# Gate and up projections in turn on chunks of 1024 tokens, in a transformer block on one Trainium2 core

## The chip, the cores and the metric

The kernel runs on one core of a Trainium2 chip (one of eight). A core has TensorE (matmuls, in the profile PE for the matmuls and PEld for their weight loads), VectorE (DVE), ScalarE (ACT), GpSimd (POOL) and SyncE (SP), which here issues all DMAs. TensorE writes only to PSUM, eight banks of 512 fp32 columns on 128 partitions; VectorE and ScalarE read them ("evict" them) into SBUF. The metric is the device time of one execution in microseconds; the median of three runs is given, and one more execution is profiled.

## What is computed

```python
xn = layernorm(x)                               # x: 2048 tokens x 576
q, k, v = xn @ wqkv                             # 32 heads of 18
s = sliding_window_attention(q, k, v, W=256) @ wo   # causal, window of 256, softmax
g = silu(((xn @ w_gate) * (xn @ w_up)) @ w_down)    # 4608 hidden columns, no nonlinearity between
return x + s * g
```

All inputs and outputs are fp32. The bilinear GLU (gate, up, their product "h", down) is the largest part of the work.

## The kernel before

**Numbers.** Each fp32 operand of a matmul is split into a high and a low fp16 part (`hi` at line 192 on ScalarE, `lo` at 195 on VectorE), and a product is three passes: high x high, high x low, low x high.

**Prologue** (up to about 179 us). Layer norm, the transposed tokens `XT`, v, then q and k; work for the loop's first weights is placed between these at negative "places".

**The loop.** 18 groups `g` of 256 hidden columns, times 4 chunks `c` of 512 tokens, make 72 slots (`NSLOT`); a slot `sl` is (g, c) and has 16 places. `seven_place(sl, place)` issues `SEVEN_N[place]` gate and up matmuls, and then `at_place` issues whatever else is due at that place. Everything else stands in the table `AT`: for each kind of step the place (counted from the first slot of the group, or from the slot), which may exceed 15 and then falls into a later slot. Each engine runs its instructions in the order in which they are issued, so the table is the schedule. Nothing is reordered at run time; an instruction that waits holds up what stands behind it on its engine, and on SP's queue a DMA that waits holds up the DMAs behind it. In one place scores come first, then down, then the rest (`RANK`).

**Gate and up by seven products.** For a 2 x 2 arrangement (two halves of the hidden columns, two halves of the tokens, two halves of the contraction) the four blocks of the result are made of seven products instead of eight (a Strassen-Winograd scheme). Weight sums are made on GpSimd (`t_sum`, line 504) and split into `TW`; sums of the tokens are made once in `s_steps` (line 536, places `AT['sx']`) into `SX` and `XD`. The units go in the order 0, 2, 1, 3, 4, 5, 6; unit 1 accumulates on the bank of 0, unit 3 on 2, 5 on 3, 6 on 4, so that a pair of banks "up" serves in turn. After each unit its bank is read (`seven_read`, line 1198): units 0 and 1 by a ScalarE copy (`seven_copy`, 1141), the others by a VectorE addition to an earlier result (`seven_add`, 1144). A unit on the same bank cannot begin before that read. The contraction of 576 leaves a tail of 64 rows; the low passes of the tails are matmuls of half the rows, two side by side (`seven_half`, 1125, at places 6 and 13).

Within a slot, a token half is 256 tokens, and each unit treats both kinds: gate in columns 0 to 255 of the bank, up in columns 256 to 511:

```python
o = slice(256 * kind, 256 * kind + 256)
nc.tensor.matmul(CH[q][:, o], a, b, start=CH["first"], ...)
```

So a matmul has 256 columns, and a slot has 92 of them, and eight of half height. At the end of a slot `seven_mult` (1148) multiplies gate by up, for each half of the hidden columns one 128 x 512 product (one on GpSimd, one on VectorE by `AT['en']`); `h_hi` (1015, ScalarE) and `h_lo` (1020, VectorE) split it, and `down` (1027) multiplies it by w_down in the next slot, in five steps of six 512-column matmuls or 24 of 64 columns, each with a VectorE addition into `acc`.

**Beside it**, slots 1 to 64 each carry one step of the attention (two heads, 512 queries): loads (`load_k`, `load_q`, `load_v`), scores (912), a masked maximum on VectorE (923), exponentials on ScalarE (935), low parts on GpSimd or VectorE (944, by `AT['en']`), a transposing DMA (947) and the weighing (956). In each group the next group's weights are loaded (`ffn_raw`, 416), their squares summed on ScalarE (`ffn_amax`, 427), the 128 partial sums spread to all partitions through DRAM (`ffn_spread_out` 436, `ffn_spread_in` 439, `ffn_scale` 447), and the weights scaled and split (`up_hi`, `up_lo`, `t_hi`, `t_lo`, `wd_*`, `dn_*`). Rings: `upw` 4 buffers, `upv` 5, `tw` 5, `hh` 4.

**End.** After slot 71 the last `down`, then `o_out` (1264) for 16 token tiles: silu, the attention's output product with wo, the product of both, the residual, the store.

## Time and profile before

| | us |
|---|---|
| median of 3 runs (1565.97 to 1566.42) | 1566.4 |
| profiled execution, its own time | 1565.05 |
| its span, first to last instruction | 1563.3 |
| busy: TensorE | 1550.1 (99%) |
| weight loads | 1107.8 (71%) |
| VectorE | 1259.1 (81%) |
| ScalarE | 1061.9 (68%) |
| GpSimd | 796.5 (51%) |
| granted TensorE clock | 1.00 throughout |

The span is from the first to the last instruction; the execution's own time has what lies around it. TensorE's busy share counts overlapping matmuls' modelled ends, so it says little of itself; the chain of waits and the waits by engine say what the end hangs on. In a row of groups stand line, engine, operation, what is written and read, shapes, count, then busy us and mean ns, then the engine's idle time just before and what ended it.

### The profile page before, as it was taken

How to read it: one execution, taken by the hardware profiler on the slowest of the kernel's cores; microseconds unless marked ns; L12 is line 12 of the kernel's file. 1: busy time of each engine (PE TensorE's matmuls, PEld its weight loads, DVE VectorE, ACT ScalarE, POOL GpSimd, SP SyncE). 2: the span in 40 equal slices, each digit the busy share in tenths (PEclk: the TensorE clock that was granted, in tenths of full speed). 3: DMA queues.
4: the chain of work that ended last, by engine and by line, in shares of the span. 5: the costliest groups of instructions: out<-in, count | busy, mean ns of one | idle time of the engine just before them, and what ended most of it. 6: DMA issues, size and time to landing. Idle time of an engine off the chain costs nothing.

```text
span 1563.3 us, 40073 instructions
## 1 busy us (share of the span) xinstructions
PE 1550.1 (99%) x15498; PEld 1107.8 (71%) x15498; DVE 1259.1 (81%) x2773; ACT 1061.9 (68%) x1854; POOL 796.5 (51%) x1015
## 2 busy tenths in 40 slices
PE   8999999999999999999999999999999999999999
PEld 5465577777777777777777777777777777777767
DVE  7536698889798989888989888888989898977655
ACT  6534487777777778787787877877778787852230
POOL 4115445546464747575756565565757474732000
PEclk9999999999999999999999999999999999999999
DMA  8683436565656686777877686877696867651238
GB/s 222 201 252 130 164 68 141 95 132 98 135 101 142 124 150 129 146 140 137 148 131 148 118 165 113 164 113 159 118 152 127 160 122 155 123 97 39 63 87 218
DMA packets 566575, 212.14 MB, mean 136 GB/s; under 512 B 504560, under 2 KB 544624, under 8 KB 566384
## 3 DMA queue, kind: packets, MB, share of 16 engines
q1 hardware_dynamic: 566384, 209.58, 64.4%
q8 instruction: 121, 1.98, 0.6%
q14 instruction: 70, 0.57, 0.1%
HBM read 76.63 MB, written 29.00 MB: 68 GB/s over the span
## 4 chain that ended last, share of the span: by engine, by line
PE 95%; DVE 1%; ACT 1%; DMA 0%; issue 0%; SPq 0%; DVEq 0%
PE up L1176 46%; PE dn L1039 25%; PE pv L956 5%; PE s L390 4%; PE up L1129 3%; PE s L912 2%; PE s L1039 2%; PE s L1279 2%; PE up L1279 2%; PE up L390 1%; PE s L341 1%; PE pv L390 1%; PE dn L390 1%; PE up L341 0%; DMA pt<-pp 0%; PE dn L341 0%
## 5 line engine op out<-in xcount | busy, mean ns | idle before, releaser
L1039 PE MATMUL dn<-dnw,hh 128*128 128x512 f16 (+1 forms) x3168 | 442.6, 286 | 0.0
L1176 PEld LDWEIGHTS <-tw 128*128 128x128 f16 x3456 | 318.1, 97 | 52.7 <-issue 4.4
L1039 PEld LDWEIGHTS <-hh 128*128 128x128 f16 x3456 | 223.2, 98 | 163.3 <-issue 19.2
L1146 DVE SCALAR_TENSOR_TENSOR gt<-up,gt 128x512 f32<-128x512 f32 x360 | 247.5, 687 | 78.2 <-PE up L1129 56.2
L1046 DVE SCALAR_TENSOR_TENSOR acc<-dn,sc,acc 128x512 f32<-128x512 f32 x310 | 215.2, 694 | 90.9 <-PE dn L1039 86.4
L931 ACT ACTIVATE mx<-mx,sig 128x2 f32<-128x2 f32 x256 | 98.1, 383 | 209.1 <-DVE mx L923 208.4
L1176 PE MATMUL up<-XT,upw 128*128 128x256 f16 x1872 | 238.6, 273 | 0.0
L1176 PE MATMUL up<-XT,tw 128*128 128x256 f16 x1728 | 234.8, 272 | 3.4 <-DVE gt L1146 3.4
L1176 PE MATMUL up<-sx,tw 128*128 128x256 f16 x1728 | 223.0, 272 | 0.0
L1176 PEld LDWEIGHTS <-upw 128*128 128x128 f16 x1872 | 178.2, 98 | 27.0 <-issue 0.2
L1151 POOL TENSOR_TENSOR ht<-gt 128x512 f32<-128x512 f32 x72 | 94.6, 1314 | 103.8 <-DVE gt L1146 102.7
L956 PEld LDWEIGHTS <-pt 128*128 128x128 f16 x2880 | 114.5, 96 | 41.8 <-DMA pt<-pp 1.6
L1176 PEld LDWEIGHTS <-upv 128*128 128x128 f16 x1152 | 105.6, 98 | 37.2 <-issue 22.0
L517 POOL TENSOR_TENSOR raw<-raw 128x256 f32<-128x256 f32 x136 | 116.6, 857 | 24.7 <-DVE upv L196 16.7
L956 PE MATMUL pv<-vt,pt 128*128 128x37 f16 x2880 | 117.8, 179 | 0.7 <-DMA pt<-pp 0.7
L1142 ACT ACTIVATE gt<-up 128x512 f32<-128x512 f32 x144 | 84.1, 584 | 49.1 <-PE up L1176 34.4
L1176 PE MATMUL up<-sx,upv 128*128 128x256 f16 x864 | 112.6, 273 | 0.0
L1017 ACT ACTIVATE hh<-ht 128x512 f16<-128x512 f32 x72 | 45.0, 625 | 37.9 <-POOL ht L1151 37.9
L196 DVE SCALAR_TENSOR_TENSOR tw<-raw,sc,tw 128x512 f16<-128x512 f32 x68 | 67.9, 999 | 0.0
L193 ACT ACTIVATE tw<-raw,sc 128x512 f16<-128x512 f32 x68 | 46.8, 712 | 27.9 <-POOL raw L517 27.9
L318 ACT ACTIVATE upw<-raw 128x1280 bf16<-128x1280 f32 (+1 forms) x51 | 62.8, 1232 | 0.5
L912 PE MATMUL s<-ks,qs 54*128 54x384 f16 (+2 forms) x512 | 60.1, 312 | 0.0
(1373 smaller groups left out, 2980.0 us busy)
## 6 DMA issues: line engine op xcount, KB each, us to landing
raw<-in_B_w_down_dram SPq DMA_DIRECT2D x36, 288.0 KB
qk_d<-qp SPq DMA_DIRECT2D x18, 512.0 KB
raw<-in_B_w_gate_dram SPq DMA_DIRECT2D x36, 256.0 KB
raw<-in_B_w_up_dram SPq DMA_DIRECT2D x36, 256.0 KB
ks<-qk_d SPq DMA_DIRECT2D x96, 81.0 KB
qs<-qk_d SPq DMA_DIRECT2D x128, 54.0 KB
vt<-v_d SPq DMA_DIRECT2D x48, 111.0 KB
qk_d<-qp SPq DMA_DIRECT2D x20, 256.0 KB
```

The lines of the kernel that those rows point to most:

```text
L196: nc.vector.scalar_tensor_tensor(w, rv, s, h, op0=OP.mult, op1=OP.subtract)
L390: nc.tensor.matmul(ps, a, b, start=i == 0 and not opened, stop=i == 12 and opened)
L517: nc.gpsimd.tensor_tensor(to, x0, x1, op=OP.subtract)
L912: nc.tensor.matmul(ps[:, :hi_ - lo_], QS[s][r, i * 128:(i + 1) * 128], KS[s][r, lo_:hi_], start=True, stop=True)
L931: nc.scalar.activation(mx[:, 1], mx[:, 0], AF.Identity, bias=sig[:, 2:3], scale=sig[:, 1:2])
L956: nc.tensor.matmul(PVB[s][:, j, i, :VW], pt[:, nb * j + n + n // nb * nb], VT[s][:, lo_ + n % nb, j * VW:(j + 1) * VW], start=n == 0, stop ...
L1039: nc.tensor.matmul(to, a, b, start=q == 0, stop=q == len(l) - 1)
L1046: nc.vector.scalar_tensor_tensor(d, src, SC[g][:, 9:10], d, op0=OP.mult, op1=OP.add)
L1142: nc.scalar.activation(seven_new(sl, name), CH[q], AF.Copy, scale=H_SC)
L1146: nc.vector.scalar_tensor_tensor(seven_new(sl, name), CH[q], H_SC, x, op0=OP.mult, op1=OP.add)
L1151: eng.tensor_tensor(HT[sl, f], u[:, 0], u[:, 1], op=OP.mult)
L1176: nc.tensor.matmul(CH[q][:, o], a, b, start=CH["first"], stop=last and q not in (1, 2, 5), skip_group_check=q in ON)
```

## The change

A slot is now (g, w, kind): a chunk `w` of 1024 tokens, and either gate (even slots) or up (odd slots). There are still 72 slots of 16 places. A token half is 512 tokens, so that a matmul has 512 columns and takes a whole bank for one kind; a slot has 46, and four of half height. A gate slot leaves its four result blocks ("11", "t", "u", "v", each 128 x 512) in tiles of their own; the up slot of the same chunk reads its block "11" from PSUM with one VectorE operation that scales it and multiplies it by the gate's (`seven_fuse`), and the other three are multiplied in SBUF (`v` and `u` on GpSimd, `t` on VectorE). `h_hi` and `h_lo` work on the four blocks; both 512-token chunks of `w` are ready after the up slot, and their downs come in the next slot (the second) and the one after (the first). After the last slot ten down steps are left.

The token sums of both 512-token parts of a 1024-token chunk go into one tile. Rings: `upw` 3, `upv` 4, `tw` 4, `hh` 5. The table `AT` has new places almost everywhere; those of which the prediction speaks are shown.

```diff
-          'en': ((0, 1, 0, 0, 0, 0, 1, 0, 0, 0), (0, 1, 0, 0, 0, 1, 1, 0, 0, 0), (0, 1, 0, 0, 0, 0, 1, 0, 0, 0),
+          'en': ((0, 1, 0, 0, 0, 0, 1, 1, 0, 0), (0, 1, 0, 0, 0, 1, 1, 0, 0, 0), (1, 1, 0, 0, 0, 0, 1, 1, 0, 0),
-          'amax': (20, 20, 13),
+          'amax': (19, 30, 6),
-          'down': ((6, 9, 12, 15, 20), (6, 8, 11, 14, 16), (6, 8, 11, 14, 16), (6, 9, 12, 15, 19)),
+          'down': ((6, 9, 12, 16, 20), (6, 8, 11, 19, 16), (6, 8, 11, 14, 16), (6, 10, 12, 15, 18)),
+          'down_last': ((11, 11, 12, 13, 11), (2, 3, 4, 5, 9)),
-          'h': (((15, 17), (18, 21)), ((17, 17), (19, 21)), ((15, 17), (21, 21)), ((15, 17), (19, 21))),
-          'load': (8, 3, 15),
+          'h': (((17, 20), (15, 16), (17, 21), (19, 20)), ((13, 14), (16, 16), (16, 18), (19, 20))),
+          'h_last': ((17, 18), (18, 19)),
+          'load': (8, 10, 15),
+          'me': (0, 1, 0),
-          'mult': {1: 6, 4: 20, 5: 1, 6: 0},
+          'mult': {4: 1, 5: 1, 6: 1},
-          'raw': (11, 11, 12, 13, -9, 2),
-          'scale': (24, 26, 36, 51),
+          'raw': (8, 10, 21, 22, -8, 0),
+          'scale': (30, 31, 38, 50),
-          't_hi': ((54, 57), (58, 65)),
-          't_lo': ((58, 59), (64, 70)),
+          't_hi': ((57, 70), (61, 74)),
+          't_lo': ((59, 73), (70, 77)),
...
-    def h_ring():
-        return post.tile([128, 2, 512], F16, name="hh", bufs=4)
+    def h_ring():
+        return post.tile([128, 2, 512], F16, name="hh", bufs=5)
...
-    def x_block(c, i, j, low):
+    def x_block(w, i, j, low, half=None):
         k = 2 * j + 5 * low
-        return XT[:, k:k + 2, c * 512 + i * 256:c * 512 + i * 256 + 256]
+        a, n = w * 1024 + i * 512, 512
+        if half is not None:
+            a, n = a + 256 * half, 256
+        return XT[:, k:k + 2, a:a + n]
...
+            for c, b in ((2 * w + 1, b + 1), (2 * w, b + 2)):
+                for n in range(5):
+                    at(min(b, NSLOT), AT["down_last"][c % 2][n] if b >= NSLOT else AT["down"][b % NCH][n], down, g, c, n)
...
+    FI = {"11": (0, 0), "t": (0, 1), "u": (1, 0), "v": (1, 1)}
...
+    def seven_half(g, c, kind, pair, stop):
+        for q, s in zip(pair, stop):
+            _, _, w, x = seven_tail(g, c, q, kind)
+            nc.tensor.matmul(CH[q], w, x, start=False, stop=s, skip_group_check=q in ON)
...
+    def seven_fuse(q, name):
+        nc.vector.scalar_tensor_tensor(GT[name], CH[q], H_SC, GT[name], op0=OP.mult, op1=OP.mult)
...
+    def seven_mult(sl, name, eng):
+        eng.tensor_tensor(GT[name], GT[name], SV[name], op=OP.mult)
...
     def seven_place(sl, place):
-        g, c = divmod(sl, NCH)
+        g, c, kind = sl // 4, sl // 2 % 2, sl % 2
...
-            o = slice(256 * kind, 256 * kind + 256)
-            nc.tensor.matmul(CH[q][:, o], a, b, start=CH["first"], stop=last and q not in (1, 2, 5),
+            nc.tensor.matmul(CH[q], a, b, start=CH["first"], stop=last and q not in (1, 2, 5),
...
+        elif q == 1:
+            if kind:
+                seven_fuse(q, "11")
+            else:
+                seven_copy(kind, q, "11")
...
-    SEVEN_N = (4, 8, 7, 6, 5, 5, 5, 4, 5, 5, 4, 6, 7, 7, 7, 7)
+    SEVEN_N = (2, 4, 4, 3, 2, 3, 2, 2, 2, 3, 2, 3, 4, 3, 4, 3)
...
-    at(NSLOT, 2, o_out, 0)
+    at(NSLOT, 8, o_out, 0)
```

More of the change, by code (lines that the diff above doesn't have):

```diff
@@ L134, in up_ring @@
     def up_ring():
-        return ring.tile([128, 10, 128], F16, name="upw", bufs=4)
+        return ring.tile([128, 10, 128], F16, name="upw", bufs=3)
     def up_ring2():
-        return ring.tile([128, 6, 128], F16, name="upv", bufs=5)
+        return ring.tile([128, 6, 128], F16, name="upv", bufs=4)
     def dn_ring():
@@ new lines @@
+    for g in range(NG):
+        for w in range(2):
+            b = 4 * g + 2 * w + 1
+            for n, name in enumerate(("v", "t", "11", "u")):
+                last = b == NSLOT - 1 and n > 1
+                for f, p in zip((h_hi, h_lo), AT["h_last"][n - 2] if last else AT["h"][w][n]):
+                    at(b, p, f, g, w, name)
+            for c, b in ((2 * w + 1, b + 1), (2 * w, b + 2)):
+                for n in range(5):
+                    at(min(b, NSLOT), AT["down_last"][c % 2][n] if b >= NSLOT else AT["down"][b % NCH][n], down, g, c, n)
```

193 lines of the change are left out of this document (89 added, 104 removed), and 30 rows, old and new, of the table AT.

## The prediction

> **What bounds the kernel now.** I read the busy shares first, then the waits of TensorE between 208 and 1480 us (the loop), then the waits of the whole span.
>
> ```profile
> span 1563.3 us, 40073 instructions
> PE 1550.1 (99%) x15498; PEld 1107.8 (71%) x15498; DVE 1259.1 (81%) x2773; ACT 1061.9 (68%) x1854; POOL 796.5 (51%) x1015
> ...
> PE pv L956 <- DMA pt<-pp: 0.7, 1, 0.7
> ...
> PE up L1176 <- DVE gt L1146: 3.4, 4, 2.1
> ```
>
> A busy TensorE proves little, since the ends of matmuls are modelled. The wait rows say more: the first, of the loop alone, is its only one, 0.7 us in 1272 us. The second is of the whole span: 3.4 us in four waits for VectorE, which lie in the opening, below. So inside the loop TensorE is the bound, and a change there is worth what it takes from TensorE's own row of instructions, unless it brings a wait. How tight that row is packed shows in the chain of waits (start, duration, what, count); the first line is from the q/k projection, the rest from the loop:
>
> ```profile
> 149.76 11.22 PE s L390 x52
> ...
> 406.72 0.33 PE up L1129 x4
> ...
> 444.62 1.29 PE dn L1039 x6
> ...
> 447.11 0.70 PE dn L1039 x24
> 447.81 3.93 PE up L1176 x36
> 451.74 0.32 PE up L1129 x4
> 452.06 0.17 PE s L912 x4
> 452.23 1.40 PE dn L1039 x6
> ...
> 479.46 0.33 PE up L1129 x4
> ```
>
> A 512-column matmul takes 11.22 us / 52 = 215.8 ns (1.29 / 6 = 215 says the same, coarser); a 256-column one 3.93 us / 36 = 109.2 ns. Two narrow ones cost 218.4 ns, so **a narrow pair costs 2.6 ns more than one wide matmul**. Read as columns plus a constant, c x 256 + k = 109.2 and c x 512 + k = 215.8: k is 2.6 ns per instruction. A weight load is not in it: 64-column matmuls with a load each follow at 0.70 / 24 = 29 ns, so a load of 128 columns fits into 29 ns and lies wholly under 109. From the halves at 406.72 to those at 479.46 are four slots: 18.2 us a slot, 1.14 us for each of its 16 places.
>
> **The change on TensorE.** The loop's up and gate instructions, counted by their weight loads:
>
> ```profile
> L1176 PEld LDWEIGHTS <-tw 128*128 128x128 f16 x3456 | 318.1, 97 | 52.7 <-issue 4.4
> ...
> L1176 PEld LDWEIGHTS <-upw 128*128 128x128 f16 x1872 | 178.2, 98 | 27.0 <-issue 0.2
> ...
> L1176 PEld LDWEIGHTS <-upv 128*128 128x128 f16 x1152 | 105.6, 98 | 37.2 <-issue 22.0
> ```
>
> With the 144 of wd (two a slot) that is 6624, 92 for each of 72 slots, as the old SEVEN_N sums to. The new one sums to 46, each of 512 columns. The half-height tails (L1129) go from four to two a call; four take 0.32 us, of which two pairs side by side are 2 x 109 and some 0.1 us is the exposed load on entering half-height rows. That 0.1 stays (the same two halves are entered), a pair becomes one of 215.8 instead of 218.4. So a slot saves (46 + 2) x 2.6 = 125 ns, and 72 slots **9.0 us**; with k taken as 2.4 or 2.8, the rounding of those rows, 8.3 to 9.7. Nothing lies over it: TensorE waits for nothing in the loop, so it comes off the end, as long as nothing else becomes late. The halved weight loads are worth nothing more, being covered by matmuls; their cover doubles.
>
> The Trainium skill ("TensorE: Matmul & The Clock Gate", section Back-to-back issue gap) gives an isolated gap of N/2.4 + 2.5 ns, near these rows, but says that a sustained stream runs at some 131 ns for N = 512; by that the sum would be 46 x (218.4 - 131) x 72 = 289 us instead of 9.0, and the row of 215.8 in a stream of 52 speaks against it.
>
> **The other engines.** Durations from the groups of 280 to 1240 us, and the load of four slots:
>
> ```profile
> L1146 DVE SCALAR_TENSOR_TENSOR gt<-up,gt 128x512 f32<-128x512 f32 x258 | 177.3, 687 | 54.4 <-PE up L1129 40.8 <-PE up L1176 7.0
> ...
> L1151 POOL TENSOR_TENSOR ht<-gt 128x512 f32<-128x512 f32 x52 | 68.7, 1322 | 27.0 <-DVE gt L1146 26.2
> L1142 ACT ACTIVATE gt<-up 128x512 f32<-128x512 f32 x104 | 60.6, 583 | 6.1 <-PE up L1176 6.1
> ...
> L1151 DVE TENSOR_TENSOR gt<-gt 128x512 f32<-128x512 f32 x52 | 41.7, 802 | 0.0
> ...
> L1023 DVE SCALAR_TENSOR_TENSOR hh<-hh,gt 128x512 f16<-128x512 f16 x52 | 35.5, 682 | 0.0
> ...
> L1017 ACT ACTIVATE hh<-gt 128x512 f16<-128x512 f32 x52 | 32.1, 617 | 0.0
> L318 ACT ACTIVATE upw<-raw 128x1280 bf16<-128x1280 f32 x26 | 33.0, 1268 | 0.4
> ...
> L944 POOL TENSOR_TENSOR pp<-sm__13529,pp 128x384 f16<-128x384 f32 x2 | 1.8, 938 | 3.5 <-DVE gt L1146 3.5
> ...
> 425.58 0.41 DVE L944 TENSOR_TENSOR pp<-sm__5965,pp 128x256 f16<-128x256 f32 x1
> ...
> 400.00:472.60 72.60, 72.60 (x769) 53.50 (x767) 61.57 (x146) 53.87 (x100) 39.12 (x56) 1.00 0.57 116
> ```
>
> Per group (four slots): evictions by addition stay 20. ScalarE copies go from 8 to 6 (-1.2 us). Products go from 4 on VectorE and 4 on GpSimd to 2 and 4, and 2 fused evictions come in, priced like the addition with the same operand places, 0.69: VectorE -1.6 + 1.4. Two subtractions of probabilities move from GpSimd to VectorE; the row at 425.58 (0.41 us for 256 columns) bounds a 384-column one between 0.4 and the 0.94 of GpSimd, I take 0.6: +1.2. VectorE goes from 61.6 to about 62.6 of 72.6 us. None of this is on TensorE's path by itself. What counts is where it stands. The fused eviction comes at place 6 of an up slot, behind the addition of unit 2, where ScalarE copied before. Its bank is wanted by unit 4, after unit 3. Cover on TensorE from the end of the halves: scores 0.17, down 1.40, unit 3 at 6 x 0.216 = 1.30, together 2.9 us; VectorE needs 2 x 0.6 (start to start, rows 185.38 and 185.98 below) = 1.2. So VectorE may come 1.7 us late before TensorE waits. Does it come late? The "L1129" part of the first row above (40.8 us, in this loop 53 slots) says no: VectorE stands idle waiting for the halves, some 0.8 us a slot. I cost the fuse at nothing; without the cover it is 0.6 an up slot, 22 us in all.
>
> The down products of a pair of 512-token blocks wait for the up slot and are issued one and two slots later. From the multiplied "v" and "t" (places 12 to 14) through ScalarE 0.6 and VectorE 0.7 to the first down at place 22 lie some eight places, 9.1 us: nothing. The raw ring of weights shrinks by one buffer each; a gate's buffers are read last in the third slot and the up weights are formed in the group's first gate slot (last low part at place 77, first use after 80, 3.4 us): nothing, while VectorE keeps within that.
>
> **The spread of the scales.** Its write is issued at place 30, right behind the last square sum (before: 24, sums at 20), the read at 31 (before 26), the reduction on VectorE at 38 (before 36).
>
> ```profile
> 421.63 0.38 SPq L178 DMA_DIRECT2D sd_f<-am  x1
> 424.19 0.34 SPq L444 DMA_DIRECT2D upv<-sd_f  x1
> 432.42 0.67 DVE L449 TENSOR_REDUCE sc<-upv 128x3 f32<-128x384 f32 x1
> SPq L444 <- DMA sd_f<-am: 45.5, 16, 4.0
> ```
>
> The read waits for the write on SP's queue, 2.8 us each (45.5 / 16), now with more of it in front of the probabilities' transposes and key loads queued behind; those at places 34 and later have slack of several places to their weighing. Place 30 to 38 is 9.1 us; square sum 1.27, write 2.6 (421.63 to 424.19), and the read may take from 2.6, as the write does, to 8.2 (the distance kept before). I take the low end, being the nearest like transfer: 6.5 of 9.1 us. At the high end (12.1) VectorE would stand 3.0 us. The raw loads move on the same queue, gate's to places 8 and 10, up's to 21 and 22, and stay 8 to 9 places ahead of their sums (before 7 to 9); query loads go from place 3 to 10 of the slot before, with 12 places (13.7 us) left to the scores, over the 8.2: nothing.
>
> **Opening and end.** Slots 0 and 1 now hold one gate and one up of 1024 tokens, with no down at all; before, slot 1 had one.
>
> ```profile
> 179.88 1.29 DVE L382 SCALAR_TENSOR_TENSOR qp<-s,qp 128x512 f16<-128x512 f32 x2 [1.67 <-ACT qp L381]
> 181.08 0.81 DVE L196 SCALAR_TENSOR_TENSOR dnw<-raw,sc,dnw 128x576 f16<-128x576 f32 x1
> ...
> 185.38 0.69 DVE L1146 SCALAR_TENSOR_TENSOR gt<-up,gt 128x512 f32<-128x512 f32 x1
> 185.98 0.68 DVE L562 TENSOR_TENSOR dnw<-dnw,XT 128x512 f32<-128x512 f32 x1
> ...
> 183.74 0.27 PE L1129 MATMUL up<-XT,upv 64*128 64x256 f16 x1
> 186.12 1.47 PE L1176 MATMUL up<-XT,tw 128*128 128x256 f16 x12 [2.11 <-DVE gt L1146]
> ...
> 189.60 1.47 PE L1176 MATMUL up<-XT,tw 128*128 128x256 f16 x12 [0.70 <-DVE gt L1146]
> ...
> 199.79 1.14 PE L1176 MATMUL up<-XT,tw 128*128 128x256 f16 x9 [0.28 <-DVE gt L1146]
> ...
> 157.18 1.30 POOL L517 TENSOR_TENSOR rqk<-raw 128x256 f32<-128x256 f32 x1
> ```
>
> Here VectorE is the bound: TensorE waits 2.11 + 0.70 + 0.28 = 3.1 us for it. I laid the new places out by hand at 0.60 an operation. Slot 0: two qp and two dnw low parts (2.7), one wd (0.4), one upv (0.5), one sx (0.6) stand before the addition of unit 2, so it starts about 184.1 against 185.4, and unit 3 near 184.8: some 1.1 us of waiting in the slot instead of 2.8. Slot 1: 14 operations of 0.6, and 4.6 of shorter ones and scores, make 13.0 us against 10.7 of TensorE: some 2.5 us of waiting, where before it was 0.3. Together 3.6 against 3.1; I take the difference as **0**, with -3 (all waiting gone) and +6 (GpSimd late in slot 0 with four t sums and four sx sums, at up to 1.3 each by the last row, before what the up slot reads) as ends.
>
> At the end two blocks' downs instead of one follow the last slot. TensorE's sum is the same; the last "u" needs 0.7 + 1.3 + 0.6 + 0.7 = 3.3 us to be ready, under four downs of block 3 (5.2 us). Zero.
>
> Sum: the profiled execution's 1565.05 us (span 1563.3 and 1.75 around it) - 9.0 = 1556.1. The runs' median, 1566.4, lies 1.35 above that execution, so **1557.4 us**.
>
> **Rivals.**
> - *VectorE becomes the bound in up slots.* Place 6 there holds addition, fused product and first down eviction. If VectorE comes over 1.7 us late, unit 4 waits for the fuse; 0.6 to 1 us in each of 36 slots is +22 to +36, and the time 1566.4 - 9.0 + 22 = 1579 or more. For: it is busy 85% of the loop. Against: it idles for the halves each slot now. It decides from 0.25 us an up slot (9.0 / 36). Chance 0.07.
> - *The scales come late.* With a read of 8.2 us VectorE stands 3.0 us at place 38, 1.7 of them covered: 1.3 x 17 = +22 - 9, 1566.4 + 13 = 1579; it decides from 1.7 + 0.5 us of lateness, where the 9.0 are gone (0.5 x 17). Chance 0.06.
> - *The opening gets longer*: +6 us, 1563.4. For: VectorE is the bound there and slot 1 loses its downs. Chance 0.10.
> - *The pair isn't dearer in the loop*, the 2.6 ns being lost in work beside it (weight loads crossing from other lines): 1566.4. Against: the x36 keep their rate between two lines' work. Chance 0.06.
>
> **How the numbers follow.** The forecast has 0.71; its own range is 1554 (opening cleared, 3 us less) to 1562 (half the opening's risk and a few scattered waits). Measurement can't tell 0.2%, 3.1 us, from no change. The opening's case, 3.0 us faster, lies on that border; I count 0.02 of it as faster. Faster: 0.71 + 0.02 = 0.73. Same: the other 0.08 and the no-gain case's 0.06 = 0.14. Slower: 0.07 + 0.06 = 0.13. The range for 8 in 10 reaches up through the opening and no-gain cases, 1553.5 to 1566.5, leaving out the slower ones.
>
> **What would show it.** The chain of a middle slot should show up matmuls at 0.216 us (x18 in 3.88), PEld about 3600 fewer instructions, and VectorE still waiting for the halves. TensorE's waits between 208 and 1480 should stay near 1 us. Wrong would be: a wait of TensorE on the fused eviction once an up slot; VectorE waiting for the spread's DMA; over 6 us of waits in the opening.

## The result, and the profile after

The changed kernel takes **1582.7 us** (median of four runs, 1581.0 to 1586.1) against 1566.2 for the kernel before, run beside it: a ratio of 1.0109 (95% interval 1.0092 to 1.0127). It is slower by 16.5 us, where 9 us less were forecast. The profiled execution has a span of 1581.2 us (before 1563.3).

The page of the changed kernel, span and busy times:

```profile
span 1581.2 us, 32793 instructions
...
PE 1549.4 (98%) x11898; PEld 769.9 (49%) x11898; DVE 1267.6 (80%) x2803; ACT 1047.0 (66%) x1818; POOL 761.7 (48%) x985
```

There are 3600 weight loads fewer, as forecast. Its chain of waits in a middle slot (start, duration, what, count):

```profile
448.57 3.88 PE up L1184 x18
452.45 0.32 PE up L1134 x2
```

That is 215.6 ns for a matmul of 512 columns, and 0.32 us for the halves: **TensorE's gain is there**. Start to start, without waits, the 3312 wide matmuls take 715 us where the 6624 narrow ones took 723, and the halves some 0.5 us less: 8.8 us together. But TensorE now waits. Its waits in the loop (208 to 1480 us; engine, line, what it waits for: us in total, times, longest):

```profile
PE pv L964 <- DMA pt<-pp: 11.2, 15, 2.3
PE up L1184 <- ACT gt L1148: 5.0, 17, 1.6
```

Before, the one such row held 0.7 us. The first row is the weighing of probabilities, waiting for a transposing DMA; the second a gate matmul whose bank ScalarE has not yet copied. The same view of 178 to 222 us, the opening, whose total was 3.1 us before and is 5.7 now (it overlaps the first: the wait of 1.6 us, at 210.9, is in both, so that 16 of the 17 belong to the loop's later groups):

```profile
PE up L1184 <- ACT gt L1148: 1.6, 1, 1.6
PE up L1184 <- DVE gu L1157: 1.4, 2, 0.9
PE up L1184 <- DVE uu L1157: 1.2, 1, 1.2
PE up L1184 <- DVE gv L1157: 1.1, 1, 1.1
```

These rows leave out waits that the trace does not put down to anyone. So I also took, for every neighbouring pair of matmuls, the distance of their starts less the distance that the same pair has where nothing waits, and added up what is left (from 40 ns on; from here on, "by starts"). By this the waits are 5.4 us before (3.5 in the opening, 1.0 in the loop, 0.9 at the end) and 31.2 after (7.5, 22.8, 0.9). 1563.3 - 8.8 + 25.8 = 1580.3, against a span of 1581.2: **the account closes to 1 us**, and the same sum gives the span of every experiment below that keeps TensorE's full clock to 2.5 us or better. The loop's waits stand in three places of each group of four slots:

| where | count, us | released by |
|---|---|---|
| third slot, weighing of the third query block | 12, 10.4 | transposing DMA |
| first slot, unit 1 (and small ones beside it) | 28, 7.0 | ScalarE's gate copy |
| first slot, weighing of the third block, and in four groups unit 3 | 10, 4.8 | transposing DMA, VectorE |

How the third-slot wait comes about shows in the chain of waits from 425 to 441 us:

```profile
430.08 1.69 POOL gu L1160
431.77 0.96 SPq L955
...
432.85 0.50 SPq L907
...
433.46 0.43 SPq L447
...
433.99 0.39 SPq L1001
...
434.48 3.99 DMA pt<-pp
...
438.51 0.47 PE pv L964 x12
```

GpSimd's product of "u" (1.69 us) stands ahead of a low part of the probabilities, for which the second transpose waits on SP's queue (L955); behind it in the same queue stand a load of v (L907), the read of the spread (L447) and a store (L1001), and only then the third transpose, whose transfer takes 3.99 us. The weighing is 0.66 us late.

And VectorE, from the middle of a group's last slot (first row) through the first half of the next group's first slot (second row); stretches in us, then their length and the busy time of PE, PEld, DVE, ACT and POOL. First the changed kernel, then the kernel before at the same point of a group:

```profile
757.69:766.98 9.29, 9.29 (x69) 4.25 (x67) 9.19 (x22) 8.16 (x15) 6.93 (x9) 1.00 0.66 143
766.98:775.82 8.84, 8.61 (x85) 4.32 (x84) 8.84 (x14) 7.74 (x14) 7.75 (x8) 1.00 0.57 113
```

```profile
753.00:762.33 9.33, 9.33 (x90) 6.24 (x89) 9.30 (x22) 6.93 (x12) 8.36 (x10) 1.00 0.63 115
762.33:772.07 9.74, 9.74 (x120) 7.64 (x119) 8.41 (x17) 7.38 (x15) 4.05 (x6) 1.00 0.99 175
```

VectorE was full at the end of a group before, too (9.30 of 9.33), but then had room (8.41 of 9.74) to catch up. Now it is full for the next half slot as well (8.84 of 8.84), while GpSimd works 7.75 us of it instead of 4.05.

### The profile page after: what moved, and what is told of

The parts are those of the page before. It is cut to its first block, busy times and chain, and to the rows that moved or that the text cites. A ratio compares the mean times of both kernels' runs of the same rounds, so it can differ in the third digit from the quotient of the medians.

```text
span 1581.2 us, 32793 instructions
## 1 busy us (share of the span) xinstructions
PE 1549.4 (98%) x11898; PEld 769.9 (49%) x11898; DVE 1267.6 (80%) x2803; ACT 1047.0 (66%) x1818; POOL 761.7 (48%) x985
## 4 chain that ended last, share of the span: by engine, by line
PE 73%; DVE 11%; DMA 6%; issue 3%; ACT 2%; POOL 2%; SPq 1%; DVEq 0%; ACTq 0%; POOLq 0%
PE up L1184 33%; PE dn L1046 18%; DMA pt<-pp 5%; PE pv L964 4%; PE s L393 4%; DVE hh L1031 3%; PE up L1134 2%; PE s L1046 2%; PE s L1292 2%; PE s L920 2%; PE up L1292 2%; PE up L393 1%; DVE gt L1160 1%; DVE acc L1053 1%; PE pv L393 1%
## 5 line engine op out<-in xcount | busy, mean ns | idle before, releaser
L1184 PE MATMUL up<-XT,upw 128*128 128x512 f16 x936 | 238.8, 379 | 5.2 <-ACT gt L1148 5.0
L1184 PE MATMUL up<-XT,tw 128*128 128x512 f16 x864 | 232.3, 378 | 4.2 <-DVE gu L1157 1.4
L1184 PE MATMUL up<-sx,tw 128*128 128x512 f16 x864 | 222.9, 378 | 0.1
L1184 PEld LDWEIGHTS <-tw 128*128 128x128 f16 x1728 | 147.4, 97 | 142.6 <-issue 9.1
L1184 PEld LDWEIGHTS <-upw 128*128 128x128 f16 x936 | 86.6, 98 | 102.6 <-issue 10.4
L964 PE MATMUL pv<-vt,pt 128*128 128x37 f16 x2880 | 120.5, 179 | 11.4 <-DMA pt<-pp 11.2
L1184 PE MATMUL up<-sx,upv 128*128 128x512 f16 x432 | 111.3, 381 | 0.0
L1160 POOL TENSOR_TENSOR gv<-gv,uv 128x512 f32<-128x512 f32 x36 | 53.5, 1487 | 62.4 <-DVE uv L1157 62.4
L1184 PEld LDWEIGHTS <-upv 128*128 128x128 f16 x576 | 49.2, 97 | 69.4 <-issue 22.1
L1160 POOL TENSOR_TENSOR gu<-gu,uu 128x512 f32<-128x512 f32 x36 | 47.5, 1320 | 19.6 <-DVE uu L1157 14.8
L1157 DVE SCALAR_TENSOR_TENSOR uu<-up,ut 128x512 f32<-128x512 f32 x36 | 24.9, 692 | 39.6 <-PE up L1134 21.6
L1134 PE MATMUL up<-XT,upv 64*128 64x512 f16 x144 | 55.7, 386 | 0.1
```

The source lines that it names most:

```text
L964: nc.tensor.matmul(PVB[s][:, j, i, :VW], pt[:, nb * j + n + n // nb * nb], VT[s][:, lo_ + n % nb, j * VW:(j + 1) * VW], start=n == 0, stop ...
L1134: nc.tensor.matmul(CH[q], w, x, start=False, stop=s, skip_group_check=q in ON)
L1160: eng.tensor_tensor(GT[name], GT[name], SV[name], op=OP.mult)
L1184: nc.tensor.matmul(CH[q], a, b, start=CH["first"], stop=last and q not in (1, 2, 5), skip_group_check=q in ON)
```

## The experiments

All are compared with the kernel before, run on the same chip beside them; the ratio is to that. The last two columns are TensorE's waits in us by starts, in the opening and in the loop.

| kernel | us | ratio (95%) | opening | loop |
|---|---|---|---|---|
| the changed kernel | 1582.7 | 1.0109 (1.0092 to 1.0127) | 7.5 | 22.8 |
| t's low part first | 1587.8 | 1.0147 (1.0130 to 1.0164) | 7.1 | 25.7 |
| attention's old places | 1603.6 | 1.0249 (1.0234 to 1.0264) | 10.4 | 42.3 |
| sum of squares earlier | 1578.7 | 1.0086 (1.0068 to 1.0104) | 10.1 | 16.3 |
| weighing later | 1574.0 | 1.0056 (1.0040 to 1.0072) | 7.3 | 13.2 |
| last slot relieved | 1578.3 | 1.0081 (1.0065 to 1.0096) | 7.3 | 17.3 |
| these last three | 1576.4 | 1.0070 (1.0052 to 1.0088) | 9.3 | 14.5 |
| weighing later, t earlier | 1574.6 | 1.0057 (1.0042 to 1.0072) | 7.1 | 14.3 |
| and last slot relieved | 1574.3 | 1.0057 (1.0042 to 1.0072) | 7.1 | 14.5 |
| opening's work ahead | 1576.0 | 1.0066 (1.0051 to 1.0081) | 6.0 | 18.6 |
| weights' sums later | 1578.4 | 1.0086 (1.0069 to 1.0103) | 7.2 | 18.8 |
| product apart, weighing later | 1585.4 | 1.0124 (1.0109 to 1.0139) | 7.3 | 24.6 |
| and sums later, opening | 1574.1 | 1.0051 (1.0034 to 1.0068) | 6.6 | 15.1 |
| and one low part behind | 1572.7 | 1.0047 (1.0033 to 1.0060) | 8.1 | 12.3 |

### Two suspects: the low part of t, and the sum of squares

```diff
-  'h': (..., ((13, 14), (16, 16), (16, 18), (19, 20))),
+  'h': (..., ((13, 17), (15, 15), (16, 18), (19, 20))),
```

> Edit: in odd chunks the split of block t (high part and low part, places 16 and 16) is done at place 15, ahead of v's low part (14, now 17). Nothing else moves. Theory 'two regular waits': in the first slot of each group TensorE waits 0.38 us (17 times, 6 us) for the gate's copy of unit 0, because its single tile is freed only by t's low part, which stands in VectorE's line behind v's; the waits should vanish and the time fall from 1582.7 to about 1577. Rival 'VectorE is the bound': its line is simply full there, the wait goes to the next bank that it reads, and the time stays within 1.5 us of 1582.7.

1587.8 us, slower still. The loop's waits now begin with:

```profile
PE up L1184 <- DVE gu L1157: 15.5, 17, 1.1
```

The 17 waits for the gate copy are gone (one of them is left), and 17 of 0.9 us stand at the next thing that VectorE owes TensorE, the read of unit 2: the wait was passed on. It also grew, by starts from 0.37 to 1.09 us a group; where the difference comes from is seen under "The wait that moves".

```diff
-  'amax': (19, 30, 6),  'scale': (30, 31, 38, 50),  'up_hi': (41, 54, 45, 60),  'up_lo': (44, 57, 50, 65),
+  'amax': (19, 34, 6),  'scale': (34, 35, 43, 50),  'up_hi': (44, 54, 46, 60),  'up_lo': (47, 57, 50, 65),
```

> Edit: the square sum of the up weights goes from place 30 to 34, the spread's write and read from 30 and 31 to 34 and 35, the reduction from 38 to 43, the first two weight splits after it 3 places later. Theory 'two regular waits': the sum stands in ScalarE's line between a score maximum and its exponentials in the second slot of each group, and the spread's write, waiting for it, holds the transposes behind it on SP's queue, so that the weighing in the third slot finds its transposed probabilities late (12 waits, 10.3 us). Those waits go, time about 1573 to 1575. Rival 'GpSimd's products': the low parts are late since u's product (1.7 us) stands ahead of them on GpSimd; then the waits stay and the time is within 2 us of 1582.7. Rival 'the wait moves': the sum now delays the exponentials of the slot after, and new waits of the same size show up one slot later.

1717.7 us, 1.096 (with the exchange of the low parts as well 1721.9, 1.100). In both one low part of gate's first weights is formed from raw weights that the first sum has already overwritten, with the same instructions. The chain of one third slot:

```profile
703.26 1.36 ACT upw L321 x2
...
704.64 2.29 DMA sd_f<-am
...
706.94 0.33 SPq L447
...
707.38 5.98 DMA pt<-pp
...
715.44 2.13 PE up L1184 x5
```

Sum of squares, write of the spread, read behind it on SP's queue, and only then the transpose that the weighing wants: four places later brought 65 us of waiting for transposes. (The last row is of the last section.) So the order of these on SP's queue can set the time; but so large a shift does not say that it does in the changed kernel. The combination says nothing more:

> Edit: e1 and e2 together. Theory 'two regular waits': their gains add up, 6 + 8 to 10 us, time about 1567 to 1569; the rest over the forecast of 1557.4 is the opening (4 us) and the late transposes in first slots (4 us). Rival 'VectorE is the bound': at most the larger one of the two gains shows.

### Attention's new places

Rows 'p' and the engines 'en' of the kernel before, in the changed kernel:

> Edit: the places of the attention's steps and the engine of their low parts are put back to those of the kernel before; all else as in the changed kernel. Theory 'two regular waits': the transposes are late for the square sum's sake and not for their own places; the waits in the third slot of each group stay, time within 3 us of 1582.7. Rival 'later transposes': the new places (second transpose 15 instead of 13, third 20 instead of 19, with the weighing where it was) made them late; the waits go, time about 1572.

1603.6 us. The waits for transposes stay (9.8 us), but the time does not, as the first theory had it, stay within 3 us: 32 waits for gate copies come to 23.0. The new places are not the fault; the old ones fit this order of work worse.

### Where the third slot's wait can be taken away

```diff
-  'raw': (8, 10, 21, 22, -8, 0),   'amax': (19, 30, 6),  'scale': (30, 31, 38, 50),
+  'raw': (8, 10, 17, 17, -8, 0),   'amax': (19, 24, 6),  'scale': (26, 29, 38, 50),
```

> Edit: up's raw weights are loaded at place 17, their square sum stands at place 24 (30 in the changed kernel) and the write and read of the spread at 26 and 29 (30 and 31); the scales are still reduced at 38 and nothing else moves. Theory A (the late square sum stands in ScalarE's line ahead of the exponentials, and its write holds up SP's queue ahead of two transposes): the twelve waits of the weighing in the third slots, 10.3 us, fall below 3 us, SP's waits for the square sum (17.6 us) fall below 6, and the time is 1573 to 1576. Theory B (the third transpose is late because of VectorE and GpSimd, the spread is not in it): the weighing's waits stay above 8 us and the time is 1580 to 1584. The gate copy's 17 waits (5.0 us) stay under both.

1578.7 us. Of the twelve waits in third slots two are left (1.0 us), with three in second slots (1.6), as theory A had it. SP's waits, first of the changed kernel (for the square sum and for the spread's write), then of this one:

```profile
SPq L181 <- ACT upw L321: 17.6, 13, 4.5
SPq L447 <- DMA sd_f<-am: 8.6, 7, 1.8
```

```profile
SPq L447 <- DMA sd_f<-am: 14.9, 15, 2.0
SPq L181 <- ACT upw L321: 11.7, 11, 2.5
```

The longest wait for the square sum falls from 4.5 to 2.5 us, and the third transpose is in time, although SP waits longer for the write. SP's total for the square sum, 11.7 us, is not below the 6 that theory A named, and the time is above its 1573 to 1576: in the first group the earlier loads and sums fall into the opening, which waits 2.6 us more.

```diff
-  (13, 14, 15, 18, 24), (13, 14, 16, 20, 24), ...   # 'p', second slots: weighing of n = 4, 5
+  (13, 14, 15, 18, 26), (13, 14, 16, 20, 27), ...
-  (13, 14, 15, 19, 26), (13, 14, 15, 21, 26), ...   # fourth slots
+  (13, 14, 15, 19, 27), (13, 14, 15, 21, 28), ...
```

> Edit: only the weighing of the third query block (n = 4, 5) moves, from places 24, 24 to 26, 27 in steps of the second slots, and from 26, 26 to 27, 28 in steps of the fourth. Theory A (a transpose comes a fixed 0.5 to 2.4 us too late for one place in the order): the weighing's waits of 14 us fall below 4 us, and the time is 1572 to 1575. Theory B (lateness is passed on: the place is late because everything behind it is late): the waits turn up again at the weighing of the last block or at the read of the result, the sum of loop waits stays above 19 us and the time above 1579. The gate copy's waits (5.0 us) stay under both.

1574.0 us, theory A: 8.7 us for moving only where TensorE takes up what comes late. Of the weighing's 11.2 us by the profile 0.6 is left, and the gate copy's row is as it was (5.0 us, 17):

```profile
PE pv L964 <- DMA pt<-pp: 0.6, 1, 0.6
```

### VectorE's line at the end of a group

Low parts of next weights out of the last slot's end:

```diff
-  'dn': ((45, 45), (48, 55), (54, 49)),  'up_hi': (41, 54, 45, 60),  'up_lo': (44, 57, 50, 65),
+  'dn': ((45, 45), (46, 47), (54, 49)),  'up_hi': (41, 48, 45, 54),  'up_lo': (44, 50, 53, 57),
```

> Edit: four of VectorE's subtractions and two of ScalarE's roundings for the next group's weights move out of the end of the group's last slot, where VectorE has no gap from place 8 of that slot to place 10 of the next: both low parts of w_down to 46 and 47 (48, 55), up's two weight pairs rounded at 48 and 54 (54, 60), with low parts at 50 and 57 (57, 65), one of gate's at 53 (50). No work is added or left out. Theory A (VectorE's line is full there, and the gate copy's wait for the buffer that the low part of t reads is its backlog): the 17 waits of unit 1 (6.5 us start to start) fall below 2 us, waits of the weighing in first slots (3.9 us) fall by half, and the time is 1573 to 1577. Theory B (the buffer's order alone makes that wait): the 17 waits stay at 0.3 us or more each and the time is 1581 to 1585.

1578.3 us, 4.4 less than the changed kernel. The gate copy's waits in first slots fall only from 7.0 to 4.7 us, and 16 new ones, 3.8 us, stand at the beginning of the fourth slot, where the moved low parts now are. The weighing's fall by 5.8. Neither theory holds as put: the waits shrink, and part of them moves. With the two other edits together:

> Edit: the three edits of the earlier square sum, the later weighing and the relieved last slot together. If they remove different waits (Theory A): loop waits fall from 23 us to about 3, and the time is 1561 to 1565, at or below the kernel before. If they are one shortage that moves from place to place (Theory B): loop waits stay above 10 us and the time is above 1570.

1576.4, theory B: 14.5 us of waits in the loop, and the opening's 9.3 through the earlier loads. The low part of t ahead of the last scores, then (place 15 in place of 16, with the later weighing), without and with the relief (here up's roundings at 47 and 54):

> Edit: the weighing of the third block later (as in the run with the later weighing, 1574.0 us), and in steps of the fourth slot the maximum over the last scores at place 16 (15), so that the low part of t in up slots of the second chunk stands at place 15 (16), ahead of it. Theory A (the gate's first copy waits only for that low part, 0.36 us late): the 17 waits of unit 1, 6 to 7 us together, vanish and the time is 1567 to 1569. Theory B (VectorE's line is full from the last slot into the first, as the earlier exchange of low parts showed): the waits turn up at the addition of unit 2 and the time stays at 1573 or more.

> Edit: the run before this one, and four low parts for the next group's weights out of the last slot's end (low parts of w_down at 46 and 47, up's at 50 and 57, one of gate's at 53; up's roundings at 47 and 54). Theory A of the run before: no further gain, 1566 to 1569. Theory B (VectorE's backlog): only here do the waits in first slots go; 1565 to 1568, at least 4 us under the run before.

1574.6 and 1574.3 us: nothing gained over the later weighing alone. In the first the gate copy still waits 0.37 us: the low part of t at the end of a group begins 0.5 us earlier, but takes 1.32 us there instead of 0.85. Its group of instructions (mean ns behind the busy us), which has the two chunks of each group together, in the first of these two:

```profile
L1031 DVE SCALAR_TENSOR_TENSOR hh<-hh,gt 128x512 f16<-128x512 f16 x26 | 26.9, 1034 | 3.5 <-ACT hh L1025 3.5
```

The same operation took 682 ns in the kernel before. In the changed kernel the four low parts stand so:

```profile
L1031 DVE SCALAR_TENSOR_TENSOR hh<-hh,gu 128x512 f16<-128x512 f16 x26 | 24.6, 947 | 0.0
...
L1031 DVE SCALAR_TENSOR_TENSOR hh<-hh,g 128x512 f16<-128x512 f16 x26 | 21.9, 843 | 0.0
...
L1031 DVE SCALAR_TENSOR_TENSOR hh<-hh,gt 128x512 f16<-128x512 f16 x26 | 20.9, 803 | 3.5 <-ACT hh L1025 3.5
...
L1031 DVE SCALAR_TENSOR_TENSOR hh<-hh,gv 128x512 f16<-128x512 f16 x26 | 20.2, 777 | 0.0
```

These are means of two kinds: in the first chunk of a group the four take 0.68 to 0.76 us, in the second, at the group's end, 0.85 (t), 0.84 (v), 1.21 (u) and 1.01 (11). What stretches them? GpSimd's sums of up's raw weights stand at the same places, so these were moved alone:

```diff
-  'sum': (..., (64, 66, 67, 70)),  't_hi': ((57, 70), (61, 74)),  't_lo': ((59, 73), (70, 77)),  'wd': ((58, 72), (65, 73), (71, 78)),
+  'sum': (..., (70, 71, 72, 73)),  't_hi': ((57, 73), (61, 75)),  't_lo': ((59, 76), (70, 78)),  'wd': ((58, 74), (65, 75), (71, 79)),
```

> Edit, on the changed kernel alone: GpSimd's four sums of up's raw weights move from places 64, 66, 67, 70 to 70 to 73, and what reads them follows (roundings 73 and 75, low parts 76 and 78, the tail's three steps 74, 75, 79). VectorE's instructions are the same in number. Theory A (VectorE's low parts of h, 0.78 to 0.95 us on average against 0.68 before, are stretched by GpSimd working on SBUF at the same time): the low parts of 11 and u fall from 0.84 and 0.95 to below 0.75, that of up's last weights from 0.84 to 0.61, the fourth weighing's waits in first slots shrink, and the time falls by 2 to 5 us, 1578 to 1581. Theory B (they are longer for another reason): the means stay and the time is 1582 to 1584.

```profile
L1031 DVE SCALAR_TENSOR_TENSOR hh<-hh,gu 128x512 f16<-128x512 f16 x26 | 17.7, 679 | 0.0
L1031 DVE SCALAR_TENSOR_TENSOR hh<-hh,g 128x512 f16<-128x512 f16 x26 | 17.6, 677 | 0.0
```

1578.4 us, and the low parts of u and 11 are back at 0.68 us with their number and sizes unchanged: **GpSimd's work on SBUF lengthens VectorE's**. (That of up's last weights, expected to fall too, went from 0.84 to 0.94: the one at the end of each group still stands beside GpSimd's low part of the probabilities, and takes 1.3 us instead of 1.1.) The Trainium skill, in "SBUF — State Buffer", section Who interferes with whom, says that a VectorE instruction with two inputs in SBUF contends with a GpSimd instruction that reads SBUF, and one with at most one such input, outside VectorE's two-port modes, does not. The trace agrees: the additions that read a PSUM bank (L1157) stay at 0.68 to 0.69 us throughout.

With the later weighing, the order of v and t exchanged, and these sums:

> Edit: the later weighing, the later sums, the low part of t ahead of that of v and of the last scores' maximum (v at 17, t at 15, scores at 16), one of up's low parts at 68 (65) and those of w_down at 50 and 52 (48, 55). The exchange of v and t alone moved the gate copy's wait to the addition of unit 2, 15.5 us. Theory A (VectorE's line there is too long by the 1.4 us that GpSimd stretches it): with the sums out of it the 17 waits for the gate copy vanish and do not come back at the addition of unit 2; loop waits below 6 us; 1565 to 1569. Theory B (the line is too long without that): waits of 0.3 us or more per group stay at one of the two, 1572 or more.

1575.6 us, 1.0067 (1.0052 to 1.0082), loop waits 16.1 (theory B). At one such place, looked at in the timeline, VectorE stood idle 0.84 us for ScalarE's rounding of t, which is behind exponentials, and then the low part took 1.27 us, begun 0.2 us behind a low part of probabilities on GpSimd.

### The wait that moves, shown in one group

The gate copy shares its buffer with the product h. So the product was written over up's block, which frees the gate's as soon as it is multiplied, and no engine's order changes:

```diff
-        eng.tensor_tensor(GT[name], GT[name], SV[name], op=OP.mult)
+        eng.tensor_tensor(SV[name], GT[name], SV[name], op=OP.mult)
```

> Edit: the later weighing (1574.0 us alone), and the three products written over up's block in place of gate's, so that the gate copy of the next group does not need the buffer which ScalarE and VectorE still split into the parts of h; nothing else moves. Theory A (the 0.36 us wait of unit 1 in first slots is for that one buffer): the 17 waits, 7.0 us with their neighbours, vanish, as does the opening's 1.8 us in slot 2, and what is left of VectorE's late line shows at the addition of unit 2 with less than 3 us: 1566 to 1569. Theory B (VectorE's line is too long by as much anyway): the waits come back at the addition of unit 2, 6 us or more, 1573 or more.

1585.4 us, **theory B**, worse than the later weighing alone by 11 us. The copy is in time, and:

```profile
PE up L1184 <- DVE gu L1157: 14.4, 17, 1.1
```

The timeline of VectorE and then of GpSimd at one such place (start, duration) shows the line that TensorE waits for:

```profile
771.37 0.85 DVE L1031 SCALAR_TENSOR_TENSOR hh<-hh,ut 128x512 f16<-128x512 f16 x1
772.15 1.08 DVE L199 SCALAR_TENSOR_TENSOR upv<-raw,sc,upv 128x384 f16<-128x384 f32 x1
773.14 0.47 DVE L1053 SCALAR_TENSOR_TENSOR acc<-dn,sc,acc 128x256 f32<-128x256 f32 x1
773.54 1.01 DVE L1031 SCALAR_TENSOR_TENSOR hh<-hh,g 128x512 f16<-128x512 f16 x1
774.47 1.21 DVE L1031 SCALAR_TENSOR_TENSOR hh<-hh,uu 128x512 f16<-128x512 f16 x1
775.60 1.27 DVE L952 TENSOR_TENSOR pp<-sm__10347,pp 128x384 f16<-128x384 f32 x1
776.79 0.68 DVE L1157 SCALAR_TENSOR_TENSOR gu<-up,gt 128x512 f32<-128x512 f32 x1
```

```profile
771.63 1.17 POOL L519 TENSOR_TENSOR raw<-raw 128x256 f32<-128x256 f32 x1
772.77 1.23 POOL L952 TENSOR_TENSOR pp<-sm__10347,pp 128x384 f16<-128x384 f32 x1
773.96 1.17 POOL L519 TENSOR_TENSOR raw<-raw 128x256 f32<-128x256 f32 x1
775.09 2.55 POOL L952 TENSOR_TENSOR pp<-sm__10351,pp 128x384 f16<-128x384 f32 x2
```

No gap, and four of the seven lengthened by 0.3 to 0.7 us each beside GpSimd (elsewhere upv takes 0.61, the low parts of h 0.68, that of the probabilities 0.55). But three of the four are as long in the changed kernel and with the later weighing. New is the low part of the probabilities just ahead of the read, 1.27 us in 16 groups. In the changed kernel it takes 0.55, and stands so to GpSimd's next one (VectorE's row, then GpSimd's):

```profile
773.59 0.55 DVE L952 TENSOR_TENSOR pp<-sm__10347,pp 128x384 f16<-128x384 f32 x1
```

```profile
774.12 1.80 POOL L952 TENSOR_TENSOR pp<-sm__10351,pp 128x384 f16<-128x384 f32 x2 [1.00 <-ACT pp L946]
```

In the changed kernel GpSimd stands idle 1.00 us for a ScalarE copy and begins 0.53 us behind VectorE. With the gate's buffer free ScalarE is earlier, GpSimd has no gap, begins 0.51 us ahead of VectorE, and VectorE's operation takes 0.72 us longer. 16 x 0.72 = 11.5 us is what this run lost against the later weighing (11.4), and 0.72 us a group is what the wait grew by in the first exchange, where the same operation takes 1.27 us too. So theory B holds for the place, but 0.72 of the 1.02 us by which the read is late in a group, by starts, is a new lengthening, and only some 0.3 (an estimate, the difference) is the wait of 0.37 passed on.

The same kernel with the sums later (and the opening's work ahead, below):

> Edit: the run before this one, with GpSimd's sums later, a low part of w_down's tail at 73 (71), and the opening's work ahead of the loop (the tail of the token sums behind its source, the last split at 17). Theory A: VectorE's low parts of h at 0.68 to 0.78 us, waits of first slots below 2 us, opening below 5 us, and 1561 to 1565, level with the kernel before or faster. Theory B (waits move on): loop waits above 10 us and 1570 or more.

1574.1 us. The waits behind unit 2 in first slots, 27 with 18.1 us in the run before, are down to less than 0.3 us, and the low part of probabilities takes 0.55 again: that line was too long by what GpSimd adds to it. But now 11 waits (about 6 us by starts) stand in second slots:

```profile
PE up L1187 <- DVE gu L1160: 4.6, 11, 0.5
```

There a low part of up's sums, moved together with them, stands just ahead of the read. It alone one place further (79), with the weighing one place later again:

> Edit, on the run before this one: the last low part of up's weight sums behind the addition of unit 6 (place 79, before 78), the third block's weighing one place later again (27 and 28; 28), and the last split of the token sums in the opening at 24 (30). Theory A (in the run before, the 11 waits of 0.56 us in second slots are for that one low part ahead of the read of unit 6): they vanish, 6.3 us, the weighing's waits fall by 2 or more, and the time is 1564 to 1567, level with the kernel before. Theory B (VectorE's line is too long in any order): the waits turn up elsewhere and the time is 1571 or more.

1572.7 us, the lowest of all, 1.0047 (1.0033 to 1.0060). These 11 are gone; the waits ahead of the downs in third slots grew from 1.5 to 4.4 us, smaller ones came in first and second slots (2.7), and the opening grew by 1.5. So theory A for the place, and theory B for the time. The intervals of this run, of the later weighing alone (1.0040 to 1.0072) and of most variants that contain it overlap: no edit beyond that one is shown to have made the kernel faster.

### The opening

```diff
+    for k in range(2):
+        for f, p in zip((dn_hi, dn_lo, dn_low), (-8, -7, -6)):
+            at(0, p + k, f, 0, k)
-  (-14, -11, -11, -10, -7, -7, -4, -3, 2, 3, 6, 6, 6, 2, 17, 17, 18),      # 'sx', third part
+  (-14, -11, -11, -10, -7, -7, -4, -6, -5, -3, -4, -3, 6, -9, -8, -7, 17),
```

> Edit, on the changed kernel: work of the opening goes ahead of the loop, where VectorE and GpSimd are idle for about half of 160 to 180 us: both low parts of w_down at places -7 and -6 (1 and 2), two of the weights' low parts at -1 (2 and 3), and nine steps of the third part of the token sums at -9 to -3 (-3 to 17). Theory A (VectorE's line is what makes TensorE wait in the first three slots): their waits fall from 7.5 us to 4 or less and the time is 1578 to 1580. Theory B (they wait for something else, or VectorE falls behind with the evictions of q and k instead): the waits stay above 6.5 us and the time is 1581 to 1585.

1576.0 us. Here, and in the first of the two runs below, a tail of the token sums is written over its source before that is split, so that parts of the sums hold other values; the instructions are the same. VectorE's load goes where it was meant to go, from 180 to 200 us into 160 to 180 (busy us, third column, 9.10 and 19.38 in the changed kernel):

```profile
160.00:180.00 20.00, 20.00 (x98) 8.65 (x96) 14.37 (x21) 9.88 (x19) 12.83 (x13) 1.00 0.44 171
180.00:200.00 20.00, 17.75 (x85) 7.55 (x84) 15.57 (x32) 10.07 (x18) 7.08 (x8) 1.00 0.48 152
```

The opening's waits fall only from 7.5 to 6.0 us: 1.8 of it is in the third slot, for a gate copy. That wait was still 1.7 with the product written apart, so it is ScalarE's line, where exponentials and a square sum stand ahead without a gap (203.9 to 210.2 us in the changed kernel). Most of the rest of the gain, 4 us, comes from the weighing's waits in the loop, which fall from 10.4 to 6.4 without a cause that I could name. Neither theory holds as put. With the later weighing, t and relief, and then in the order of v and t exchanged (tail behind its source):

> Edit: the second and the third of these runs together (later weighing, earlier low part of t, relieved last slot, opening). If the waits found are the whole of what was lost (Theory A): loop waits under 6 us, opening under 4, and 1560 to 1564, faster than the kernel before by 1 to 5 us. If the gain of 9 us on TensorE was not there or the waits only move (Theory B): 1568 or more.

> Edit: the run before this one, with the opening's work ahead of the loop (as in the earlier opening run, with the tail of the token sums behind its source, at -1 and 0, and the last split at 8). Theory A (the whole loss is in the loop's waits and in the opening's): 2 to 5 us under the run before it, 1561 to 1566, level with the kernel before or faster. Theory B (opening not repaired by VectorE's order): within 1.5 us of the run before it.

1573.3 (1.0047, 1.0030 to 1.0063) and 1577.3 us (1.0081, 1.0065 to 1.0097). The second is level with its base (1575.6; the runs of the two overlap): the opening has a new wait of 2.9 us, for a read of unit 4 by VectorE. Neither is theory A's.

## Why the prediction was wrong

**Right.** The matmuls, step by step: 215.6 ns a piece, the halves, 3600 loads less, 9.0 us forecast and 8.8 found. The fused eviction at nothing: TensorE waits for it nowhere. VectorE still waits for the halves. The scales: VectorE does not stand still for the spread's read; that rival did not happen.

**Near by luck.** VectorE's total: +1.0 us a group were forecast, 8.5 us over 17 groups, 0.5 each, were found. The terms are other ones: the low parts of h cost 1.3 us a group more than priced, and that of up's last weights (upv) 0.4; against them the low parts of the weights' sums (tw) fell from 1.02 to 0.82 us each, 0.8 a group, and seven subtractions of probabilities now take no longer than five before. What stands beside GpSimd changed, and with it what is lengthened.

**Wrong, the largest term, 10.4 us:** "those at places 34 and later have slack of several places to their weighing" (the spread of the scales). The third transpose is issued at place 36 and was wanted at 40, 4.6 us later; its transfer alone takes 3.99 us. I had counted the queue's own DMAs but not that ScalarE's square sum, now at place 30, stands ahead of the exponentials, that GpSimd's product stands ahead of a low part, and that both arrive at the same queue. Taking away either side, the sum's lateness or the early weighing, took that wait away (1.0 us left in third slots, and 0.6 in all by the profile). The product's part in it is read from one chain; it was not taken away by itself.

**Wrong, 7.0 us and a part of 4.8 in first slots:** "None of this is on TensorE's path by itself. What counts is where it stands", and then I looked only at place 6 of the up slots, and took the idle time of VectorE as a mean over slots. At the end of a group there is none. The prediction's buffers were those of the weights; the gate's own tile, one buffer that is read by ScalarE, multiplied, and read again by VectorE before the next gate copy, was not looked at. That buffer carried the wait: with the product apart the copy is in time, and the next read of VectorE's line is late instead.

**Wrong in size:** the low parts of h priced at the 682 ns of the kernel before. They measured 777 to 947. With two of each in a group that is 1.3 us a group, and 1.2 of it falls on the four at the group's end, whose new places lie beside GpSimd's work, in a line of 8.8 us that has no gap. Moving the sums away brought those of u and 11 back to 0.68 and, with the product apart, took away the first slots' waits behind unit 2.

**Wrong, 4.0 us:** the opening's difference of 0. I had worked out 1.1 us for slot 0 and 2.5 for slot 1; they were 2.3 and 2.1. The third slot, 3.0 us, was not in the sum at all. The sign named for this, over 6 us of waits in the opening, came true by starts (7.5), not by the profile's rows (5.7 to 222 us).

**The rivals.** "VectorE becomes the bound in up slots" named the engine and a time that fits (1579 or more), but not the place: it is the gate slot at the start of a group, not the fuse, and VectorE is only a part of the cause. That the time fits is chance. The chance for slower, 0.13, was far too small for a change that moved nearly every entry of a table in which VectorE was already full at one point of each group.

**Open.** Whether an order exists that keeps the 8.8 us; and how much of a wait in VectorE's line is passed on when only one operation moves, since GpSimd's work shifts with it. Of the variants none has less than 12 us of waits in the loop, and none beats the kernel before; in most, a part of what was taken away came back at the next thing that VectorE or the queue owed. That is shown for single waits, not that it must be so.

## What to carry to other kernels

Where a bound engine has no wait and the others are 80% busy, price a new order by the fullest stretch of each helper engine, not by its mean idle time: list its instructions in a row over that stretch, with what shares its buffers and queue behind it. A wait removed from a full line turns up at the next thing that the line owes; make the line shorter, or let the consumer come later, before changing who waits. Durations from the old kernel hold only while the same neighbours run beside them: compare the mean of a group of instructions with its shortest one, and look at what runs beside the long ones.

## What the hardware showed that was not expected

- A VectorE operation with both inputs in SBUF takes 0.68 us for 128 x 512 fp16 and up to 1.32 us while GpSimd works on SBUF: the rows above, and the two that fell back to 0.68 when GpSimd's sums moved. Which begins first counts: a subtraction of 128 x 384 took 0.55 us where it began 0.53 us ahead of GpSimd's, and 1.27 where GpSimd's had begun 0.51 us earlier.
- TensorE's granted clock was halved after a wait of 3.8 us. In the run with the later square sum, stretches of 4 us (PE busy in the second, granted clock in the third column from the end):

```profile
705.00:710.00 5.00, 4.44 (x38) 2.01 (x34) 4.42 (x11) 3.86 (x8) 1.79 (x2) 1.00 0.34 29
710.00:714.00 4.00, 0.60 (x13) 0.51 (x14) 0.80 (x3) 1.61 (x3) 1.78 (x2) 0.79 1.19 190
714.00:718.00 4.00, 4.00 (x16) 1.56 (x15) 1.08 (x2) 0.00 (x0) 0.00 (x0) 0.50 0.85 130
```

  Matmuls of 512 columns then take 426 ns (2.13 us for five at 715.44 in its chain, quoted above), and in that run 54 us more of waiting for transposes than in the changed kernel went with 135 us more of time. The Trainium skill, "TensorE: Matmul & The Clock Gate", section What's actually happening, has the clock at half rate after an idle window of about 3.4 us; the trace agrees.
